# Attention and mixture of experts in one kernel: scaling of the values moved behind the gate products, list writes of the third batch put later, two gathers a step apart

## The chip, the cores and the metric

One core of a Trainium2 chip runs the whole kernel. The metric is device time in microseconds of one execution: 571.93 us is the median of three runs before the change (571.28 to 574.95). A profiled execution of the same kernel took 578.27 us; all durations below are from it.

## The reference

```python
# attention: batch 4, heads 8, seq 768, head_dim 64, n_global 8, n_local 96
scores = scale * q @ k.T                                  # per batch and head
rel    = pos[:, None] - pos[None, :]
keep   = (pos[None, :] < n_global) | ((rel >= 0) & (rel < n_local))
scores = where(keep, scores - slopes * dist, -1e9)
a      = exp(scores - max);  a = a / (sum(a) + 1e-9)
x      = (a @ v)  ->  rows of 3072 tokens x 512

# mixture of experts, one expert of 8 for each token (D 512, F 1024)
logits = x @ w_gate + modality_bias[modality_id]
e_idx  = argmax(logits);  gate_w = softmax(logits)[e_idx]
for e in range(8):
    out[e_idx == e] = gate_w * (relu(x[e_idx == e] @ w1[e]) @ w2[e])
```

The expert's matmuls run in a split form (high and low parts of both operands, three matmuls for one product).

## The kernel before, in words

The tokens are 24 blocks of 128 rows, six for each batch. The attention is a software pipeline over them: `step(n)` (L1091) works on five blocks at once. In order of TensorE's instructions it does the scores of block n in two halves (`s_mm`, L214), the transposes of block n−1's probabilities in four groups pt_0 to pt_3 (`t_mm`, L259) with a copy out of PSUM for each (`t_cp`, L266 on ScalarE, L268 on VectorE), the product with the values of block n−2 (`pv`, L280 and L292), the gate products of block n−4 (`gate_b`, L339), the transpose of block n−3's rows (`gate_a`, L330), and the sum of the gate's four quarters for block n−4 (`gate_c`, L348, added up by VectorE at L349).

Between these, VectorE finds the maxima of the scores (`mx`, eight instructions of L230, four for each half) and ScalarE takes the exponentials (`ex`, L246). `rinv` (L301 to 307) inverts the sums of the rows, which PV puts into a column beside its values, and `xr` (L310 to 323) scales the values of PV with them, out of PSUM into `xr`, and sends the rows to HBM (`x_rows`, SP's queue). PV's two PSUM tiles for a block (`x`, pool pX) have room behind the values, and `gate_b` and `gate_c` put their results there: the gate products of block n−4 go into the tile of block n−2.

At the end of each batch the routing follows, by a table of functions and steps (`at(step, function, ...)`, L999 to 1010): `route_a` makes the one-hot choice of experts, `route_b` (L376) counts tokens with two matmuls, copies the counts (`pks`, L386) and lets POOL (VectorE for the last batch) add up bases and positions (L389 to 395), `route_d` (L398) makes the reciprocal of the gate sum and turns positions into row numbers (`pf` L404, `pi` L406), and `route_c` (L409) writes one block's tokens into the sorted list in HBM (`ids_sorted`), six indirect DMAs from POOL for a batch. For the first two batches (BE = 2) they are spread over the steps, one each, behind a ScalarE instruction of the step; for the others they come together. What the table gives to steps past the attention is run by `rest()` (L1167), a generator from which `fill` takes one piece at every second turn of the first three expert units.

The experts are 14 units: three with tokens of the first two batches alone (`e0` to `e2`), eight of 256 rows (`s`) and three of 128 (`g`) with what is left. Those of the first two batches can start when the attention ends, since their lists are planned from step 17 on (`plan_e`); weights of `e0` are loaded from step 18 (LAST) on and split into high and low parts in steps 20 to 23 (`split`: ScalarE L623, VectorE L624). `ld_x` reads a unit's list (`uie`, in step 22), `gather_x` (L587) gathers its rows with two indirect DMAs from POOL (`xge`), `x_t` (L627) transposes them, and the first matmul of `e0` (L652) follows the gates of the last blocks.

What sets the order: TensorE, ScalarE and VectorE are in an order written out by hand during the attention (L1073 to 1076), TensorE and ScalarE also among the experts. POOL, SP, and VectorE's work from `rest()` on are placed by a scheduler that runs a model of the program; it can set such an instruction between others that stand ahead of it in the code.

Of the kernel before, what the change touches and what calls it, by code (L numbers as in the profile page):

```python
# [26 lines left out]
NBLK = NT // P  # L27
NG0, NL0 = 8, 96
NB = S // P
# [8 lines left out]
BE = 2  # L38
# [13 lines left out]
GE = 2  # L52
# [7 lines left out]
def bc(ap, n):  # L60
    return ap.unsqueeze(2).broadcast_to([ap.shape[0], ap.shape[1], n])
# [7 lines left out]
def moe_attention_kernel(ctx, tc, q, k, v, qs, ks, vr, vo32, n_global, n_local, modality, w_gate, mod_bias, w1, w2, out):  # L69
# [8 lines left out]
    def p_p(name):  # L78
        return psum.tile([P, 512], F32, tag="pP", name=name, bufs=2)
# [44 lines left out]
    def copyv(n):  # L124
        i, r = n % NB, n % NV
        nc.gpsimd.tensor_copy(vo[n % 3][0:64], va[r][0:64])
        if i:
            nc.gpsimd.tensor_copy(vo[n % 3][64:P], va[(n - 1) % NV][64:P])
# [94 lines left out]
    def mx(n, hh):  # L223

        if n not in blk:
            blk[n] = gp.tile([P, H], F32, tag="nmx", name=f"nmx{n}", bufs=3)
        nmx = blk[n]
        hp, h = hh // 2, hh % 2
        sc = pp.tile([P, W], F32, tag="sc", name=f"sc{n}_{hh}", bufs=8)
        V.tensor_tensor_reduce(  # L230
            out=sc,
            in0=pss[n, hp // 2][h][:, hp % 2 * W : (hp % 2 + 1) * W],
            in1=(tbl0 if n % NB == 0 else tbl)[:, hh, :],
            op0=ALU.add,
            op1=ALU.min,
            scale=-0.125,
            scalar=3.0e38,
            accum_out=nmx[:, hh : hh + 1],
        )
        scs[n, hh] = sc  # L240
# [13 lines left out]
    def t_mm(n, hp):  # L254

        pr = prs[(NP * n + hp) % NPR]
        tp = p_p(f"pt{n}_{hp}")
        for j, o in enumerate((0, P, PRW - P)):
            nc.tensor.transpose(tp[:, j * P : (j + 1) * P], pr[:, o : o + P], ident)  # L259
        pts[n, hp] = tp  # L260

    def t_cp(n, hp, act=False):
        tp = pts[n, hp]
        pT = pp.tile([P, 3, P], F32, tag="pT", name=f"pT{n}_{hp}", bufs=4)
        if act:
            last[0] = nc.scalar.copy(pT.rearrange("p a b -> p (a b)"), tp[:, 0 : 3 * P])  # L266
        else:
            V.tensor_copy(pT.rearrange("p a b -> p (a b)"), tp[:, 0 : 3 * P])  # L268
        pts[n, hp] = pT

    pxs = {}
# [29 lines left out]
    def rinv(n):  # L301

        rin = gp.tile([P, H], F32, tag="rin", name=f"rin{n}")
        for h in range(2):
            rows = pxs[n][h][:, 0 : NP * D1].rearrange("p (a d) -> p a d", d=D1)
            V.tensor_scalar_add(rin[:, h:H:2], rows[:, :, D], 1e-9)
        V.reciprocal(rin, rin)
        blk[n] = rin

    def xr(n):  # L310
        b, i = n // NB, n % NB
        px, rin = pxs[n], blk.pop(n)
        xv = gp.tile([P, DM], F32, tag="xr", name=f"xr{n}", bufs=3)
        xrs[b, i] = xv
        for h in range(2):
            V.tensor_tensor(  # L316
                xv.rearrange("p (a h d) -> p a h d", h=2, d=D)[:, :, h, :],
                px[h][:, 0 : NP * D1].rearrange("p (a d) -> p a d", d=D1)[:, :, 0:D],
                bc(rin[:, h:H:2], D),
                ALU.mult,  # L320
            )
        t0 = n * P
        nc.sync.dma_start(xd[t0 : t0 + P, :], xv)
# [20 lines left out]
    def gate_c(b, i, lq, o=NP * D1):  # L344

        if i == 0:
            lgts[b] = gp.tile([P, NB, E], F32, tag="lgt", name=f"lgt{b}")
        nc.tensor.matmul(lq[:, o : o + E], gt.pop((b, i)), sel, start=True, stop=True)  # L348
        V.tensor_add(lgts[b][:, i, :], lq[:, o : o + E], tbias[:, b * NB + i, :])  # L349
# [231 lines left out]
    def ld_x(s):  # L581
        n = P * s.halves
        so = nc.sync.value_load(s.o_src, min_val=0, max_val=E * NT)
        s.ui = idp.tile([P, 2, 2], I32, tag="ui", name=f"ui{s.name}")
        nc.sync.dma_start(s.ui[:, 0 : s.halves, :], ids[ds(so, n), 0:2].rearrange("(t p) o -> p t o", p=P))

    def gather_x(s):  # L587
        s.xg = xgp.tile([P, 2, DM], F32, tag="xg", name=f"xg{s.name}")
        for t in range(s.halves):
            nc.gpsimd.indirect_dma_start(  # L590
                out=s.xg[:, t, :],
                out_offset=None,
                in_=s.xsrc,
                in_offset=bass.IndirectOffsetOnAxis(ap=s.ui[:, t, 0:1], axis=0),
            )
# [295 lines left out]
    def at(n, f, *args):  # L891
        todo.setdefault(n, []).append((f, args))
# [106 lines left out]
    LAST = NBLK - NB  # L999
    spaced = {}  # L1000
    for b in range(B):
        n0 = b * NB
        at(n0 + NB + 3, route_a, b)
        at(n0 + NB + 4, route_b, b)
        at(n0 + NB + 4, route_d, b)
        for j in range(NB):
            if b < BE:
                spaced[n0 + NB + 5 + j] = (b, j)
            else:
                at(n0 + NB + 5, route_c, b, j)  # L1010
    at(1, consts_a)
    at(1, consts_l)
    at(2, consts_m)
# [21 lines left out]
    eslots, slist, grs = [], [], []  # L1035
# [26 lines left out]
    at(LAST, lambda: ld_w(eslots[0], "a", (0, 1)))  # L1062
    at(LAST + 1, lambda: ld_w(eslots[0], "a", (2, 3)))
    at(LAST + 4, lambda: [ld_x(s) for s in eslots])
    at(LAST + 5, lambda: [gather_x(s) for s in eslots[:GE]])
    for j in range(4):
        at(LAST + 2 + j, split, None, "a", j)
    at(LAST + 5, lambda: ld_w(eslots[0], "b"))
# [9 lines left out]
    def load(n):  # L1078

        if n + 3 < NBLK:  # L1080
            load_kq(n + 3)
        if n + LV < NBLK:
            loadv(n + LV)

    def gates(n):
        return n // NB, n % NB
# [4 lines left out]
    def step(n):  # L1091

        on, back = n < NBLK, 0 < n <= NBLK
        load(n)
        if on:
            s_mm(n, 0)
        if back:
            t_mm(n - 1, 0)
        if on:
            s_mm(n, 1)  # L1100
            for hh in (0, 2, 1, 3):
                mx(n, hh)
                ex(n, hh)
        if back:
            t_cp(n - 1, 0)
            t_mm(n - 1, 1)
            t_cp(n - 1, 1, True)
        if n in spaced:
            route_c(*spaced.pop(n), last[0])
        if on:  # L1110
            for hh in (4, 6, 5, 7):
                mx(n, hh)
                ex(n, hh)
        if n > 1:
            pv(n - 2)
            rinv(n - 2)
            xr(n - 2)
        if n > 3:
            gate_b(*gates(n - 4), pxs[n - 2][0])
        if back:  # L1120
            t_mm(n - 1, 2)
            t_cp(n - 1, 2, True)
        if n > 2:
            gate_a(*gates(n - 3))
        if back:
            t_mm(n - 1, 3)
            copyv(n - 1)
        if n > 3:
            gate_c(*gates(n - 4), pxs[n - 2][1])
        for f, args in todo.pop(n, []):  # L1130
            if f is split:
                args = (eslots[0],) + args[1:]
            if f is route_b:
                args += (pxs[n - 2][1],)
            f(*args)
        if back:
            t_cp(n - 1, 3)
        pxs.pop(n - 2, None)

    for n in range(NBLK + 1):  # L1140
# [95 lines left out]
    for u in range(nslot):  # L1236
        s = order[u]
# [137 lines left out]
```

## Time and profile before

| | us |
|---|---|
| median of three runs | 571.93 (571.28 to 574.95) |
| the profiled execution | 578.27 |
| its span, first to last instruction | 576.5 |
| attention, to the first expert matmul | 0 to 261.9 |
| experts and end | 261.9 to 576.5 |
| TensorE busy | 503.4 (87%) |
| VectorE busy | 319.2 (55%) |
| ScalarE busy | 283.3 (49%) |
| POOL busy | 137.6 (24%) |
| mean granted TensorE clock | 0.881 of full |

The span is 1.8 us shorter than the execution's time. Shares are means over two stages with different limits: in the attention five engines hand work around, among the experts TensorE works nearly without a break. A busy time of TensorE says nothing of its speed; the granted clock has to be read beside it. The steps begin, by the first score matmul of each (step 2 to step 23): 12.9, 18.8, 26.3, 35.5, 44.3, 56.4, 65.3, 74.8, 86.9, 96.4, 107.8, 116.7, 126.2, 138.2, 147.2, 157.2, 169.5, 179.1, 189.3, 198.4, 207.9, 220.5.

### The profile page before, as it was taken

The page shows a single profiled execution, that of the slowest core. Times are in us where ns is not written, and L with a number is a line of the kernel's source. Part 1 is how long each engine was busy: PE and PEld are TensorE (multiplying, and loading weights), DVE is VectorE, ACT ScalarE, POOL GpSimd, SP SyncE. Part 2 cuts the span into 40 slices and gives each one's busy share as a digit, 9 for nine tenths or more (in the row PEclk, how much of TensorE's full clock was granted, in tenths as well). Part 3 has the DMA queues.
Part 4 walks back from the last instruction along what each step waited for, and adds up shares of the span by engine and source line. Part 5 has one row for each costly group of instructions (what it writes and reads, how often), then busy time and mean ns, then how long its engine had stood idle before and what let it go on. Part 6 is the DMA issues. An engine that isn't in the chain of part 4 may idle for free.

```text
span 576.5 us, 14334 instructions
## 1 busy us (share of the span) xinstructions
PE 503.4 (87%) x5597; PEld 437.4 (76%) x5597; DVE 319.2 (55%) x971; ACT 283.3 (49%) x523; POOL 137.6 (24%) x198
## 2 busy tenths in 40 slices
PE   7869788788886884579999999998999999999990
PEld 6757677676665764468898998987898899889980
DVE  6763535544456551334978656574658565856430
ACT  6553533544435551323654555564547555865420
POOL 8211102211322115410133032152033303230100
PEclk9995857876769766559999999999999999999997
DMA  8695532534435416212857677587668867696100
GB/s 274 215 308 185 152 124 89 162 116 131 137 111 169 162 51 203 95 67 70 290 162 250 207 261 243 194 306 254 222 217 281 300 205 252 233 324 188 69 21 22
DMA packets 59396, 105.52 MB, mean 183 GB/s; under 512 B 9615, under 2 KB 23335, under 8 KB 59320
## 3 DMA queue, kind: packets, MB, share of 16 engines
q1 hardware_dynamic: 54552, 91.47, 49.2%
q0 software_dynamic: 4768, 13.05, 6.1%
q8 instruction: 46, 0.75, 0.5%
q14 instruction: 30, 0.25, 0.1%
HBM read 90.13 MB, written 14.63 MB: 182 GB/s over the span
## 4 chain that ended last, share of the span: by engine, by line
PE 59%; DVE 14%; issue 13%; DMA 5%; ACT 3%; POOL 2%; SPq 0%; POOLq 0%; ACTq 0%; DVEq 0%; another core or an unknown queue 0%
PE pt L259 9%; PE s L214 6%; PE phs L654 4%; PE phs L652 4%; PE phs L653 4%; PE x L280 3%; DMA uig<-ids_sorted 3%; DVE sc L230 3%; PE x L292 3%; DVE pT L268 3%; PE pos L696 3%; PE pos L695 3%; PE pos L694 3%; PE phe L652 2%; PE phe L653 2%
## 5 line engine op out<-in xcount | busy, mean ns | idle before, releaser
L246 ACT ACTIVATE pr<-sc,nmx 128x168 f32<-128x168 f32 x192 | 67.6, 423 | 64.1 <-DVE nmx L230 63.1
L259 PE MATMUL pt<-ident,pr 128*128 128x128 f32 x288 | 66.2, 352 | 18.8 <-DVE pT L268 14.7
L653 PE MATMUL phs<-xls,ahs 128*128 128x256 f32 x256 | 72.2, 282 | 1.3 <-DVE xls L639 1.3
L654 PE MATMUL phs<-xhs,als 128*128 128x256 f32 x256 | 72.6, 284 | 0.6 <-DVE als L624 0.5
L652 PE MATMUL phs<-xhs,ahs 128*128 128x256 f32 x256 | 72.2, 282 | 0.0
L259 PEld LDWEIGHTS pt<-ident,pr 128*128 128x128 f32 x288 | 37.7, 171 | 32.8 <-issue 17.7
L590 POOL DMA_INDIRECT xgs<-x_rows,uis x16 | 30.2, 1888 | 133.8 <-DMA uis<-ids_sorted 79.4
L230 DVE CUSTOM_DVE_ANT_0 sc<-s,tbl 128x168 f32<-128x168 f32 x192 | 52.2, 327 | 8.8 <-PE s L214 7.6
L214 PE MATMUL s<-kt,qt 64*64 64x128 f32 (+1 forms) x1536 | 56.2, 295 | 0.5 <-DMA kt<-in_ks 0.4
L214 PEld LDWEIGHTS s<-kt,qt 64*64 64x64 f32 x1536 | 50.2, 166 | 6.8 <-issue 5.7
L694 PE MATMUL pos<-bhs,hhs 128*128 128x512 f32 x128 | 51.4, 401 | 0.0
L696 PE MATMUL pos<-bhs,hls 128*128 128x512 f32 x128 | 50.6, 395 | 0.0
L268 DVE COPY pT<-pt 128x384 f32<-128x384 f32 x48 | 26.5, 553 | 43.4 <-PE x L292 43.4
L695 PE MATMUL pos<-bls,hhs 128*128 128x512 f32 x128 | 50.5, 395 | 0.0
L412 POOL DMA_INDIRECT ids_sorted<-tki,pi x24 | 25.1, 1044 | 105.7 <-ACT pr L246 51.5
L653 PEld LDWEIGHTS phs<-xls,ahs 128*128 128x128 f32 x256 | 48.8, 191 | 1.9 <-DVE xls L639 1.6
L654 PEld LDWEIGHTS phs<-xhs,als 128*128 128x128 f32 x256 | 48.8, 191 | 1.3 <-DVE als L624 1.3
L659 DVE SCALAR_TENSOR_TENSOR hls<-phs,hhs 128x512 fp32r<-128x512 f32 x32 | 22.1, 692 | 49.0 <-ACT hhs L658 49.0
L652 PEld LDWEIGHTS phs<-xhs,ahs 128*128 128x128 f32 x256 | 48.9, 191 | 0.4
L266 ACT COPY pT<-pt 128x384 f32<-128x384 f32 x48 | 22.9, 478 | 47.7 <-PE x L292 33.4
L658 ACT ACTIVATE hhs<-phs 128x512 fp32r<-128x512 f32 x32 | 19.1, 598 | 51.9 <-PE phs L654 43.4
L339 PE MATMUL x<-xT,wg 128*32 128x128 f32 x184 | 11.8, 335 | 35.4 <-DVE xr L316 33.0
(338 smaller groups left out, 1189.0 us busy)
## 6 DMA issues: line engine op xcount, KB each, us to landing
va<-in_vr SPq DMA_DIRECT2D x25, 260.0 KB
qt<-in_qs SPq DMA_DIRECT2D x24, 256.0 KB
x_rows<-xr SPq DMA_DIRECT2D x24, 256.0 KB
kt<-in_ks SPq DMA_DIRECT2D x20, 288.0 KB
vl<-in_vo SPq DMA_DIRECT2D x50, 81.2 KB
rawe0a<-in_moe_w SPq DMA_DIRECT2D x4, 512.0 KB
rawe0b<-in_moe_w SPq DMA_DIRECT2D x4, 512.0 KB
rawe1a<-in_moe_w SPq DMA_DIRECT2D x4, 512.0 KB
```

The source lines that it names most:

```text
L214: nc.tensor.matmul(ps[h][64 * half : 64 * half + 64, c : c + cnt], qt[hs, hp, 64 * half : 64 * half + 64], keys, start=True, stop=True,)
L230: V.tensor_tensor_reduce(out=sc, in0=pss[n, hp // 2][h][:, hp % 2 * W : (hp % 2 + 1) * W], in1=(tbl0 if n % NB == 0 else tbl)[:, hh, :], o ...
L246: last[0] = nc.scalar.activation(pr[:, h * (PRW - W) : h * (PRW - W) + W], scs.pop((n, hh)), AF.Exp, bias=blk[n][:, hh : hh + 1], scale=-1.0,)
L259: nc.tensor.transpose(tp[:, j * P : (j + 1) * P], pr[:, o : o + P], ident)
L268: V.tensor_copy(pT.rearrange("p a b -> p (a b)"), tp[:, 0 : 3 * P])
L590: nc.gpsimd.indirect_dma_start(out=s.xg[:, t, :], out_offset=None, in_=s.xsrc, in_offset=bass.IndirectOffsetOnAxis(ap=s.ui[:, t, 0:1], axi ...
L652: nc.tensor.matmul(o, hi[:, fs], s.xh[:, c, :], start=(c == 0), stop=False)
L653: nc.tensor.matmul(o, hi[:, fs], s.xl[:, c, :], start=False, stop=False)
L654: nc.tensor.matmul(o, lo[:, fs], s.xh[:, c, :], start=False, stop=(c == 3))
L694: nc.tensor.matmul(s.po[t], s.hh[:, fc, tt], hi[:, wv], start=(fc == 0), stop=False)
L695: nc.tensor.matmul(s.po[t], s.hh[:, fc, tt], lo[:, wv], start=False, stop=False)
L696: nc.tensor.matmul(s.po[t], s.hl[:, fc, tt], hi[:, wv], start=False, stop=(fc == 7))
```

## The change

```diff
@@ the table
-        at(n0 + NB + 4, route_d, b)
+        at(n0 + NB + 4 if b < BE else max(n0 + NB + 4, NBLK + 1), route_d, b)
...
-                at(n0 + NB + 5, route_c, b, j)
+                at(max(n0 + NB + 5, NBLK + 1), route_c, b, j)
...
-    at(LAST + 5, lambda: [gather_x(s) for s in eslots[:GE]])
+    for j in range(GE):
+        at(LAST + 5 + j, lambda j=j: gather_x(eslots[j]))
@@ step(n)
         if n > 1:
             pv(n - 2)
-            rinv(n - 2)
-            xr(n - 2)
         if n > 3:
             gate_b(*gates(n - 4), pxs[n - 2][0])
         if back:
             t_mm(n - 1, 2)
-            t_cp(n - 1, 2, True)
+            t_cp(n - 1, 2)
         if n > 2:
             gate_a(*gates(n - 3))
         if back:
             t_mm(n - 1, 3)
+            t_cp(n - 1, 3, True)
             copyv(n - 1)
         if n > 3:
             gate_c(*gates(n - 4), pxs[n - 2][1])
+        late = []
         for f, args in todo.pop(n, []):
             if f is split:
                 args = (eslots[0],) + args[1:]
             if f is route_b:
-                args += (pxs[n - 2][1],)
+                f(*args, pxs[n - 2][1])
+            else:
+                late.append((f, args))
+        if n > 1:
+            rinv(n - 2)
+            xr(n - 2)
+        for f, args in late:
             f(*args)
-        if back:
-            t_cp(n - 1, 3)
```

So in each step: `rinv` and `xr` of block n−2 come behind the gate's work instead of ahead of it; the copy of pt_2 goes from ScalarE to VectorE and that of pt_3 from VectorE to ScalarE, right behind its transposes; of the routing, `route_b` stays ahead of `rinv`, and the rest of the step's table comes behind `xr`. For the third batch, `route_d` goes from step 22 and `route_c` from step 23 to step 25, which is past the attention and so in `rest()`. The gather of `e1` goes from step 23 to step 24. The last block's code behind the loop is as it was.

VectorE at the end of step 6, before: the last of eight maxima, `rinv` and `xr` of block 4, the gate's sum, the copy of pt_3, and the next step's first maximum.

```order
L230 ISA sc_7_1114,nmx_1084<-s_1_1_1067,tbl_161 128x168
L230 ISA nmx_1084 128x1
L306 TENSOR_SCALAR rin_1151<-x_0_1117 128x4
L306 TENSOR_SCALAR rin_1151<-x_1_1118 128x4
L307 RECIPROCAL rin_1151<-rin_1151 128x8
L316 TENSOR_TENSOR xr_1155<-x_0_1117,rin_1151 128x4x64
L316 TENSOR_TENSOR xr_1155<-x_1_1118,rin_1151 128x4x64
L349 TENSOR_TENSOR lgt_867<-x_1_1118,tbias 128x8
L268 COPY pT_3_1187<-pt_3_1178 128x384
L230 ISA sc_0_1236,nmx_1235<-s_0_0_1195,tbl 128x168
```

And now:

```order
L230 ISA sc_7_1114,nmx_1084<-s_1_1_1067,tbl_161 128x168
L230 ISA nmx_1084 128x1
L268 COPY pT_2_1161<-pt_2_1157 128x384
L349 TENSOR_TENSOR lgt_861<-x_1_1118,tbias 128x8
L306 TENSOR_SCALAR rin_1180<-x_0_1117 128x4
L306 TENSOR_SCALAR rin_1180<-x_1_1118 128x4
L307 RECIPROCAL rin_1180<-rin_1180 128x8
L316 TENSOR_TENSOR xr_1184<-x_0_1117,rin_1180 128x4x64
L316 TENSOR_TENSOR xr_1184<-x_1_1118,rin_1180 128x4x64
L230 ISA sc_0_1236,nmx_1235<-s_0_0_1195,tbl 128x168
```

The copy and the gate's sum have come ahead of `rinv` and `xr`; the copy is that of pt_2.

VectorE at the end of step 22, before: the gate's sum, the third batch's counts (`pks`), its reciprocals, `pf` and `pi`, a split of `e0`'s weights, the copy of pt_3, the next step's first maximum.

```order
L349 TENSOR_TENSOR lgt_3759<-x_1_3693,tbias 128x8
L386 COPY pks_3764<-x_1_3693 128x96
L400 TENSOR_REDUCE se_3777<-ex_3601 128x6
L401 TENSOR_SCALAR se_3777<-se_3777 128x6
L402 RECIPROCAL tki<-se_3777 128x6
L404 TENSOR_REDUCE pf_3781<-pos_3773 128x6
L406 CAST pi_3783<-pf_3781 128x6
L624 TENSOR_TENSOR ale_3819<-rawe0a_3290,ahe_3818 128x1024
L268 COPY pT_3_3822<-pt_3_3753 128x384
L230 ISA sc_0_3865,nmx_3864<-s_0_0_3824,tbl 128x168
```

And now, at the end of the step after it, step 23, where `pf` and `pi` of the third batch stand, up to the copy of pt_0 in step 24:

```order
L268 COPY pT_2_3933<-pt_2_3929 128x384
L349 TENSOR_TENSOR lgt_3753<-x_1_3890,tbias 128x8
L306 TENSOR_SCALAR rin_3952<-x_0_3889 128x4
L306 TENSOR_SCALAR rin_3952<-x_1_3890 128x4
L404 TENSOR_REDUCE pf_4248<-pos_3767 128x6
L307 RECIPROCAL rin_3952<-rin_3952 128x8
L406 CAST pi_4250<-pf_4248 128x6
L316 TENSOR_TENSOR xr_3956<-x_0_3889,rin_3952 128x4x64
L316 TENSOR_TENSOR xr_3956<-x_1_3890,rin_3952 128x4x64
L624 TENSOR_TENSOR ale_3964<-rawe0a_3294,ahe_3963 128x1024
L268 COPY pT_0_3979<-pt_0_3975 128x384
```

`pf` and `pi` have moved by one step, into the middle of `rinv` and `xr` of block 21; the reciprocals have gone to step 21.

POOL from the last copy of values to the gather of `e2`, before:

```order
L128 COPY vo_80<-va_76 64x520
L590 DMA xge_3972<-x_rows,uie_3794 128x512 x2
L590 DMA xge_3975<-x_rows,uie_3805 128x512 x2
L389 TENSOR_TENSOR base<-base,pks_3764 128x8 x6
L393 TENSOR_TENSOR pos_3773<-pks_3764,base 128x48
L391 COPY base<-base 128x8
L394 TENSOR_TENSOR pos_3773<-pos_3773,ebase 128x48
L395 TENSOR_TENSOR pos_3773<-pos_3773,oh_3607 128x48
L412 DMA ids_sorted<-tki,pi_3783 24832x16 x6
L590 DMA xge_4295<-x_rows,uie_3816 128x512 x2
```

And now:

```order
L128 COPY vo_80<-va_76 64x520
L389 TENSOR_TENSOR base<-base,pks_3758 128x8
L590 DMA xge_3960<-x_rows,uie_3788 128x512 x2
L590 DMA xge_4058<-x_rows,uie_3799 128x512 x2
L389 TENSOR_TENSOR base<-base,pks_3758 128x8 x5
L393 TENSOR_TENSOR pos_3767<-pks_3758,base 128x48
L391 COPY base<-base 128x8
L394 TENSOR_TENSOR pos_3767<-pos_3767,ebase 128x48
L395 TENSOR_TENSOR pos_3767<-pos_3767,oh_3609 128x48
L412 DMA ids_sorted<-tki,pi_4250 24832x16 x6
L590 DMA xge_4277<-x_rows,uie_3810 128x512 x2
```

One of the six sums of bases has gone ahead of the four gathers; the gathers of `e0` and `e1` still stand together, and the six list writes where they stood.

## Rows read from the trace of the kernel before

**Rows 1.** The page's second part, one row: the TensorE clock that was granted in 40 equal slices of the span (14.4 us each), in tenths of full speed (9 is 90% or more).

```profile
PEclk9995857876769766559999999999999999999997
```

**Rows 2.** The table by stretches: stretch and its length in us, busy us and (instructions) of each engine, granted clock as a share of 2.4 GHz, mean busy share of the DMA engines, GB/s. Steps 2 to 4; steps 5 to 21; from step 23's scores to the first expert matmul; the experts.

```profile
12.80:35.40 22.60, 17.74 (x441) 14.60 (x439) 15.81 (x81) 13.48 (x37) 5.30 (x9) 1.00 0.78 246
35.40:207.80 172.40, 140.24 (x2625) 118.23 (x2623) 84.98 (x467) 79.12 (x207) 35.73 (x64) 0.76 0.47 147
220.40:261.90 41.50, 25.52 (x332) 20.75 (x332) 12.64 (x46) 9.01 (x21) 14.53 (x22) 0.59 0.40 135
261.90:566.00 304.10, 298.70 (x1872) 265.44 (x1871) 191.71 (x298) 166.98 (x217) 68.25 (x50) 1.00 0.64 214
```

**Rows 3.** Who waited for whom: engine, line waited at, what ended the wait: us in total, times, longest us. Two rows of TensorE's waits from 0 to 262 us, and one of VectorE's from the whole span.

```profile
PE x L339 <- DVE xr L316: 33.0, 19, 3.8
PE pt L259 <- DVE pT L268: 14.7, 8, 8.3
...
DVE pf L404 <- POOL pos L395: 13.4, 3, 8.9
```

**Rows 4.** Timeline of TensorE at the end of step 4 and in step 5, mostly at full clock: start in us from the span's start, duration in us, engine, line, operation, tiles (out<-in), shape, count, and in brackets the idle time before it and what ended it. Scores `s`, first PV group `x` (L280), gate products (L339), third transpose group `pt` of the step's second half, next step's scores.

```profile
33.35 0.43 PE L339 MATMUL x<-xT,wg 128*32 128x128 f32 x8 [1.80 <-DVE xr L316]
...
35.48 0.91 PE L214 MATMUL s<-kt,qt 64*64 64x128 f32 x32
...
38.12 0.70 PE L280 MATMUL x<-vl,pT 40*64 40x65 f32 x32
...
41.70 0.43 PE L339 MATMUL x<-xT,wg 128*32 128x128 f32 x8 [1.80 <-DVE xr L316]
...
43.23 0.90 PE L259 MATMUL pt<-ident,pr 128*128 128x128 f32 x3 [0.19 <-ACT pT L266]
...
44.29 0.51 PE L214 MATMUL s<-kt,qt 64*64 64x128 f32 x4
```

**Rows 5.** Timeline of VectorE and ScalarE in the same step 5: first score row `sc`, copy `pT` of pt_0 on VectorE and of pt_1 on ScalarE, the second four exponentials `pr`, `rinv` and `xr`, the copy `lps`.

```profile
37.44 0.32 DVE L230 CUSTOM_DVE_ANT_0 sc<-s,tbl 128x168 f32<-128x168 f32 x1
...
39.25 0.56 DVE L268 COPY pT<-pt 128x384 f32<-128x384 f32 x1 [0.72 <-PE x L292]
...
39.53 0.48 ACT L266 COPY pT<-pt 128x384 f32<-128x384 f32 x1 [0.31 <-PE x L292]
...
40.09 1.41 ACT L246 ACTIVATE pr<-sc,nmx 128x168 f32<-128x168 f32 x4
...
40.73 0.22 DVE L306 TENSOR_SCALAR rin<-x 128x4 f32<-128x4 f32 x2
...
41.22 0.76 DVE L316 TENSOR_TENSOR xr<-x,rin 128x256 f32<-128x256 f32 x2
...
42.20 0.27 ACT L341 COPY lps<-x 128x128 f32<-128x128 f32 x1 [0.70 <-PE x L339]
```

**Rows 6.** Timeline of TensorE in a step at half clock, step 9: its scores, its gate products, the next step's scores.

```profile
74.81 1.55 PE L214 MATMUL s<-kt,qt 64*64 64x128 f32 x32
...
83.72 0.65 PE L339 MATMUL x<-xT,wg 128*32 128x128 f32 x8 [1.21 <-DVE xr L316]
...
86.89 0.51 PE L214 MATMUL s<-kt,qt 64*64 64x128 f32 x4
```

**Rows 7.** Timeline of VectorE in step 10, the routing of the first batch: the copy `pks`, and `pf`, which reads POOL's positions.

```profile
96.54 0.26 DVE L386 COPY pks<-x 128x96 f32<-128x96 f32 x1 [0.33 <-PE x L384]
...
99.58 0.20 DVE L404 TENSOR_REDUCE pf<-pos 128x6 f32<-128x48 f32 x1 [2.24 <-POOL pos L395]
```

**Rows 8.** Timeline of steps 22 and 23: step 22's scores; the last list write of the second batch, first and last of four gathers, the last of the third batch's position sums; `pf`, a weight split and the copy of pt_3 on VectorE; the transposes on TensorE that use its tile.

```profile
207.87 1.55 PE L214 MATMUL s<-kt,qt 64*64 64x128 f32 x32
...
216.08 0.98 POOL L412 DMA_INDIRECT ids_sorted<-tki,pi  x1 [8.90 <-ACT pr L246]
...
222.87 1.00 POOL L590 DMA_INDIRECT xge<-x_rows,uie  x1 [3.42 <-DMA uie<-ids_sorted]
...
226.69 0.95 POOL L590 DMA_INDIRECT xge<-x_rows,uie  x1 [0.30 <-issue]
...
230.00 0.28 POOL L395 TENSOR_TENSOR pos<-pos,oh 128x48 f32<-128x48 f32 x1
230.31 0.20 DVE L404 TENSOR_REDUCE pf<-pos 128x6 f32<-128x48 f32 x1 [8.94 <-POOL pos L395]
...
230.72 1.23 DVE L624 TENSOR_TENSOR ale<-rawe0a,ahe 128x1024 fp32r<-128x1024 f32 x1
...
231.86 0.55 DVE L268 COPY pT<-pt 128x384 f32<-128x384 f32 x1
...
232.56 0.87 PE L259 MATMUL pt<-ident,pr 128*128 128x128 f32 x3 [8.35 <-DVE pT L268]
```

**Rows 9.** Timeline of the attention's end: pt_2 of the last block on TensorE, the last `rinv` on VectorE, the first expert matmul.

```profile
252.38 0.90 PE L259 MATMUL pt<-ident,pr 128*128 128x128 f32 x3
...
261.33 0.23 DVE L306 TENSOR_SCALAR rin<-x 128x4 f32<-128x4 f32 x2 [3.09 <-ACT lps L341]
...
261.92 0.36 PE L652 MATMUL phe<-xhe,ahe 128*128 128x256 f32 x1
```

**Rows 10.** Timeline among the experts: the gather of the first unit of the last plan on POOL, and the first transposes that use it.

```profile
309.72 0.98 POOL L590 DMA_INDIRECT xgs<-x_rows,uis  x1 [14.25 <-DMA uis<-ids_sorted]
...
329.55 0.60 PE L635 MATMUL mts<-ident,xgs 128*128 128x128 f32 x4
```

## The prediction

> **What bounds the kernel now.** I read the clock row of the page first, then a table by stretches, then who TensorE waited for, and last one step of the attention instruction by instruction. In the clock row [rows 1] the reader sees full clock (2.4 GHz) in the first slices, a mixture from the fourth to the eighteenth, and full clock again from then on. The table [rows 2] puts names to it: the mixture of experts (261.9 to 566) has TensorE busy 298.7 of 304.1 us at a granted clock of 1.00, so nothing but fewer matmuls would shorten it, and the change takes none away. The attention runs at 0.76, and its end, 220.4 to 261.9, has TensorE busy for 25.5 of 41.5 us. So all that can be won lies ahead of 262 us. There TensorE's largest wait is for `xr` of VectorE, 33.0 us in 19 times, 1.74 each [rows 3]: the gate products (L339) write the PSUM tile that `xr` reads.
>
> One step at full clock [rows 4]: step 5 starts at 35.48, its gate products start at 41.70 after a wait of 1.80, and from gate products to the next step's scores it took 2.13 in the step before (33.35 to 35.48). That is 6.22 + 2.13 = 8.35 us. (Step 5 itself took 8.81, since the clock fell in its last part.) A step at 1.2 GHz [rows 6] takes 12.08 with a wait of 1.21, so 10.9 without. The 17 steps from 35.48 to 207.87 take 172.4 us, 10.14 each: a mixture of the two.
>
> **The change part by part.** *`rinv` and `xr` behind the gate products.* No instruction is added or dropped; a PSUM copy changes engines with another of the same size (0.56 on VectorE, 0.48 on ScalarE [rows 5]). TensorE's own order stays, and the wait of 1.80 goes, since the tile that the gate products write has no reader yet. What is late next, in step 5 counted from 35.48: PV ended at 4.42 (41.70 less 1.80). The last transpose group, pt_3, needs pt_2's copy; that now stands on VectorE behind the second four score rows, which end at 5.25 (40.73), so it is done at 5.81. TensorE gets there by itself at 4.42 + 1.34 = 5.76 (41.70 to 43.23 less the old wait of 0.19): no loss. gate_c needs the copy `lps`, which stands on ScalarE behind four exponentials that end at 6.02 (41.50), so it is there at 6.29; 0.3 for gate_c, and the next step's scores start at some 6.65 instead of 8.35. I take 6.9, for hand-overs between engines that I cannot see. Bounds: 6.65, and 8.9 if the clock stays a mixture (10.14 less 1.74, plus 0.5 for the new waits).
>
> The clock is the larger half of this. Before it fell, at the end of step 5, TensorE had stood still 1.80 and 0.19 us in one step [rows 4]; from 12.8 to 35.4 it kept 1.00 with TensorE busy 17.7 of 22.6 us [rows 2]. A step of 6.65 would hold some 0.3 us of waiting, a fuller engine than in that stretch. So I expect full clock in most steps. Bounds: never falling, or the mixture as before.
>
> `xr` then ends 1.25 us (40.73 to 41.98) after gate_c's sum, at about 8.2, that is 1.5 into the next step; VectorE's next score rows come at 2.0 of that step (37.44 against 35.48 by the same spacing), so VectorE is not late. Its DMA, `x_rows`, is 1.2 us later, and the loads behind it on SP's queue with it; they are made one to three steps ahead, and the traffic of 147 GB/s [rows 2] becomes some 216 at 6.9 us a step, below the 246 that the first steps drew.
>
> Steps with more work cost more. In steps 10 and 16 VectorE waits for POOL's positions: 13.4 us in three, less 8.9, makes 2.2 each [rows 3], and from `pks` to `pf` it takes 3.0 [rows 7]. `pks` now stands ahead of `rinv`, so about 1 us of waiting is left, but score rows follow at once: 0.17 + 3.04 + 0.4 after 6.9 puts them at 10.5 instead of 8.7; I take 2.0 a step. Steps 9, 15, 20, 21 have routing sums or a weight split of 1.23 on VectorE behind `xr`: 1.0 each. And I let the clock fall twice after such steps, each for a step's length: 10.9 less 6.9, 4.0 each. Sum of the 17 steps: 117.3 + 4 + 4 + 8 = 133.3, a gain of 39.1. Step 4 adds its wait, 1.7.
>
> *Third batch's list writes.* Before, VectorE's `pf` in step 22 stood from 221.3 to 230.3 for POOL, whose position sums lay behind four gathers that waited for the list [rows 8]; the transposes behind it started only at 232.56. In the new order `pf` is gone from step 22, but not from the attention: the scheduler puts it into step 23, between that step's `rinv` and `xr`. On POOL nothing moves: gathers, sums and six list writes stand as they did, except that one of six sums goes ahead of the gathers. What then comes late, from step 22's start (207.87 before): the list write waits for ScalarE's copy, done at 4.5 (40.01 in step 5), 4.6; the list is read back 6.8 later (216.08 to 222.87), 11.4; from there to the last position 7.4 (230.28), 18.7. VectorE gets to `pf` at 7.8 (step 22 with its split) + 7.1 = 14.9 and waits 3.8. Then `pf`, reciprocal, `pi`, `xr` and the split, about 2.9 with their hand-overs, and the copy of pt_0, 0.5: 22.1, which step 24's pt_2 needs. From pt_2 to the first expert matmul it was 252.38 to 261.92 [rows 9], 9.5 at mostly half clock; I take 8.4 (at full clock it would be near 6). First expert matmul at 30.5 instead of 54.05 (207.87 to 261.92): a gain of 23.5. Bounds: 27 if `pf` waits for nothing, 36 if it waits 8.9 as before.
>
> *Gathers a step apart.* POOL has them back to back in both orders: nothing.
>
> *Behind the attention.* The route of the third batch takes two more turns of the planner, 5 us at 1.3 a piece. The first list of the last plan was gathered at 309.72 and used at 329.55 [rows 10], so this hides; I charge 1.0. A split of 1.23 has come ahead of the last `rinv` on VectorE, in a chain at the end of the attention: 1.0.
>
> Sum: 39.1 + 1.7 + 23.5 − 2.0 = 62.3. The profiled execution took 578.27 us, 6.3 above the median of 571.93; it becomes 516.0, and the median about 510.
>
> **The rivals.** *The clock keeps swinging.* For it: from 35.4 to 207.8 it did so in every step or two, and after the change short waits for copies remain in each. Against it: the stretch at 1.00 named above. Price: 8.9 a step gives 17 × 1.24 = 21.1 (its extras are in the 10.14), step 4 1.7, the end 4 less, 19.5, and −2: a gain of 40.3, 532 us. The Trainium skill tells of such a case (TensorE: Matmul & The Clock Gate, "A second HAM failure mode: psum-queue depth-cycling"): where PSUM buffers turn over in each iteration, small idles between groups of matmuls keep the clock swinging. By that rule the change would leave the swing, as its tiles still turn over each step, and the time would be this rival's; the trace bears it out from 35.4 on, and not from 12.8 to 35.4.
>
> *The third batch's part does not do what it says.* `pf` in step 23 may wait as long as it did in step 22. For it: POOL's order is the same. Against it: VectorE comes to it a step later. Price: 36 instead of 30.5, 515 us.
>
> *Slower.* The place is the PSUM pair of PV: a step's PV may start only when `xr` of two steps before has read it. By my reckoning `xr` ends 1.5 into a step and PV starts at 2.64 (38.12 less 35.48), 1.1 to spare; before, at full clock, 4.5 (8.35 + 2.64 less 6.50, where `xr` ended). `rinv` now waits for ScalarE's `lps` too, as it did for 3.09 us in the one place where the old order had it so [rows 9]. If `xr` came d late, each of 18 steps would grow by d less 1.1. The gain of 62 is used up at d = 4.6; at 5.2 the time is 571.9 − 62.3 + 18 × 4.1 = 583. Nothing in the rows holds `lps` that long.
>
> **How the numbers follow.** A measurement of this kernel can tell about 1% from no change. Forecast 0.62; swinging clock 0.20 (532); long `pf` 0.12 (515); slower 0.03 (583); no change that can be told 0.03. Low end: 17 × 6.65 without falls of the clock saves 12.3 more, the end at 27 saves 3.5: 494. High end: the swinging clock, 532, with 2 for hand-overs: 534. Faster is 0.94, within 1% 0.03, slower 0.03.
>
> **What would show it.** Right: TensorE's wait for `xr` is gone from the list; a plain step takes about 7 us; the clock row shows nines to the end of the attention, with a lower slice or two; step 22's `pf` is gone and one in step 23 waits some 4 us; the first expert matmul comes near 200 us; the stretch of the experts is as long as before to 3 us. Wrong: PV waits for `xr`; fives in the clock row; TensorE idle among the experts for a list that comes late.

## The result and the profile after

The changed kernel takes 496.02 us (median of 4 runs, 494.71 to 499.26), the one before took 573.44 in the same session: ratio 0.866, interval 0.861 to 0.872. Taken a second time, in another session (c1 below), it took 496.16 us, 0.867 (0.863 to 0.871). The profiled execution took 494.71 us, with a span of 492.9 us; the span before was 576.5.

The clock row of the page, of the changed kernel (a slice is 12.3 us), to be set beside [rows 1]:

```profile
PEclk9999999999999899999999999999999999999995
```

The fives to eights of before are gone but for one slice (the last one is where the work runs out). The table by stretches, with the columns of [rows 2]: steps 2 to 4, steps 5 to 21, from step 22's scores to the first expert matmul (in [rows 2] this stretch starts a step later, with step 23's scores), the experts:

```profile
12.80:32.20 19.40, 17.89 (x441) 14.73 (x439) 15.04 (x77) 13.08 (x36) 5.11 (x9) 1.00 0.78 249
32.20:149.80 117.60, 110.47 (x2625) 90.23 (x2623) 84.10 (x467) 73.25 (x207) 35.17 (x63) 1.00 0.69 218
149.80:181.00 31.20, 24.91 (x489) 19.84 (x489) 20.25 (x82) 16.63 (x39) 17.68 (x28) 0.89 0.55 188
181.00:485.00 304.00, 297.86 (x1871) 265.11 (x1870) 191.60 (x297) 165.55 (x215) 67.91 (x50) 0.99 0.64 216
```

The reader sees the same number of matmuls in steps 5 to 21 (2625) in 117.6 us instead of 172.4, at a clock of 1.00 instead of 0.76; TensorE is busy for 94% of it. By parts, in us:

| part of the span | before | after | gain | predicted |
|---|---|---|---|---|
| up to step 5's scores | 35.48 | 32.28 | 3.2 | 1.7 |
| steps 5 to 21 | 172.39 | 117.61 | 54.8 | 39.1 |
| step 22's scores to the first expert matmul | 54.05 | 31.02 | 23.0 | 23.5 |
| experts to the end | 314.6 | 312.0 | 2.6 | −2.0 |
| span | 576.5 | 492.9 | 83.6 | 62.3 |

TensorE's waits over the whole span (line waited at, what ended it: us in total, times, longest), to be set beside [rows 3]:

```profile
PE pt L259 <- DVE pT L268: 8.4, 26, 1.3
PE x L280 <- DVE xr L316: 3.6, 1, 3.6
```

The 33.0 us at the gate products have no row any more. What is left is mostly 0.2 to 0.3 us a time for copies (the longest 1.3), and one wait of PV for `xr`. A plain step of the changed kernel, that is one without routing, planning or weight splits on VectorE, is step 14; on TensorE (scores, PV, gate products, pt_3, next scores), against [rows 4]:

```profile
92.92 0.91 PE L214 MATMUL s<-kt,qt 64*64 64x128 f32 x32
...
95.56 0.70 PE L280 MATMUL x<-vl,pT 40*64 40x65 f32 x32
...
97.27 0.42 PE L339 MATMUL x<-xT,wg 128*32 128x128 f32 x8
...
98.82 0.55 PE L259 MATMUL pt<-ident,pr 128*128 128x128 f32 x3 [0.21 <-DVE pT L268]
...
99.46 0.91 PE L214 MATMUL s<-kt,qt 64*64 64x128 f32 x32
```

and on VectorE the first instructions that it does within this step (`rinv` and `xr` of the step before), and its copy of pt_2, against [rows 5]:

```profile
93.11 0.22 DVE L306 TENSOR_SCALAR rin<-x 128x4 f32<-128x4 f32 x2
...
93.61 0.76 DVE L316 TENSOR_TENSOR xr<-x,rin 128x256 f32<-128x256 f32 x2
94.28 0.32 DVE L230 CUSTOM_DVE_ANT_0 sc<-s,tbl 128x168 f32<-128x168 f32 x1
...
98.21 0.56 DVE L268 COPY pT<-pt 128x384 f32<-128x384 f32 x1
```

The step is 6.54 us long (99.46 less 92.92) with one wait of 0.21. `xr` ends 1.45 into it (94.37), PV, which needs the PSUM pair that `xr` reads, starts at 2.64: 1.2 to spare. The one long wait stands in the attention's end (before: [rows 8, 9]):

```profile
165.22 0.95 POOL L590 DMA_INDIRECT xge<-x_rows,uie  x1 [0.30 <-issue]
165.26 0.22 DVE L306 TENSOR_SCALAR rin<-x 128x4 f32<-128x4 f32 x2
...
168.52 0.20 DVE L404 TENSOR_REDUCE pf<-pos 128x6 f32<-128x48 f32 x1 [3.04 <-POOL pos L395]
...
169.28 0.76 DVE L316 TENSOR_TENSOR xr<-x,rin 128x256 f32<-128x256 f32 x2 [0.28 <-DVE pi L406]
169.76 1.46 PE L280 MATMUL x<-vl,pT 40*64 40x65 f32 x32 [3.60 <-DVE xr L316]
...
180.91 0.36 PE L652 MATMUL phe<-xhe,ahe 128*128 128x256 f32 x1
```

`pf`, which stands between `rinv` and `xr`, waits for POOL, whose last gather and sums come first; PV waits for `xr`. PV's 32 matmuls then take 1.46 instead of 0.70: the clock is at half from 167.8, within the wait, to 174.6, the only time between 32 and 181 us.

### The profile page after: what moved, and what is told of

Read it like the earlier page. It is cut to its first block, busy times and chain, and to the rows that moved or that the text cites. A ratio compares the mean times of both kernels' runs of the same rounds, so it can differ in the third digit from the quotient of the medians.

```text
span 492.9 us, 14301 instructions
## 1 busy us (share of the span) xinstructions
PE 460.7 (93%) x5597; PEld 398.3 (81%) x5597; DVE 318.6 (65%) x971; ACT 276.9 (56%) x523; POOL 137.5 (28%) x198
## 4 chain that ended last, share of the span: by engine, by line
PE 56%; DVE 16%; issue 14%; DMA 6%; ACT 3%; POOL 3%; SPq 1%; POOLq 0%; DVEq 0%
PE pt L259 6%; PE s L214 5%; PE phs L654 5%; PE phs L652 4%; PE phs L653 4%; DVE sc L230 4%; DVE pT L268 4%; DMA uig<-ids_sorted 4%; PE pos L696 3%; PE pos L695 3%; PE pos L694 3%; PE phe L652 2%; PE x L280 2%; PE phe L653 2%; PE phe L654 2%
## 5 line engine op out<-in xcount | busy, mean ns | idle before, releaser
L259 PE MATMUL pt<-ident,pr 128*128 128x128 f32 x288 | 52.5, 292 | 10.1 <-DVE pT L268 8.4
L659 DVE SCALAR_TENSOR_TENSOR hls<-phs,hhs 128x512 fp32r<-128x512 f32 x32 | 22.1, 692 | 49.4 <-ACT hhs L658 49.4
L259 PEld LDWEIGHTS pt<-ident,pr 128*128 128x128 f32 x288 | 30.0, 141 | 23.0 <-DVE pT L268 15.1
L214 PE MATMUL s<-kt,qt 64*64 64x128 f32 (+1 forms) x1536 | 44.0, 250 | 0.7 <-DMA kt<-in_ks 0.4
L214 PEld LDWEIGHTS s<-kt,qt 64*64 64x64 f32 x1536 | 38.5, 132 | 5.7 <-issue 4.5
L710 POOL DMA_INDIRECT out<-obs,ois x16 | 16.1, 1006 | 47.4 <-ACT obs L709 44.4
```

The source lines that it names most:

```text
L214: nc.tensor.matmul(ps[h][64 * half : 64 * half + 64, c : c + cnt], qt[hs, hp, 64 * half : 64 * half + 64], keys, start=True, stop=True,)
```

## The experiments

Theory A: the wait of TensorE for `xr` in each step cost twice, by itself and by the clock that fell after it; the move of `rinv` and `xr` takes both away; the rest of the change is worth a few us. Rivals: the third batch's part carries the gain (B), the exchange of the copies does (C), the clock's fall has nothing to do with the wait (D). From e5 on the letters are those of each run's own expectation.

**e1_step_only: the changed step, the rest as before.**

```diff
-        at(n0 + NB + 4 if b < BE else max(n0 + NB + 4, NBLK + 1), route_d, b)
+        at(n0 + NB + 4, route_d, b)
-                at(max(n0 + NB + 5, NBLK + 1), route_c, b, j)
+                at(n0 + NB + 5, route_c, b, j)
-    for j in range(GE):
-        at(LAST + 5 + j, lambda j=j: gather_x(eslots[j]))
+    at(LAST + 5, lambda: [gather_x(s) for s in eslots[:GE]])
```

Expected: 

> The changed step (scaling behind the gate products, the copies of pt_2 and pt_3 exchanged) with the table of the routing and the gathers as before the change. Theory A (TensorE's standing still for xr in each step costs its own length and, through the clock, as much again): plain steps of 6.5 us at full clock as in the changed kernel, pf back in step 22 with a wait of 7 to 9 us: 502 us. Theory B (the gain comes from the third batch's part): 540 us or more, plain steps of 9 us.

Measured: 500.19 us (498.68 to 504.64), ratio 0.873 (0.868 to 0.878). A plain step takes 6.54. Its end, timeline of VectorE and TensorE:

```profile
162.69 0.43 PE L339 MATMUL x<-xT,wg 128*32 128x128 f32 x8
...
168.55 0.20 DVE L404 TENSOR_REDUCE pf<-pos 128x6 f32<-128x48 f32 x1 [8.13 <-POOL pos L395]
...
171.71 0.90 PE L259 MATMUL pt<-ident,pr 128*128 128x128 f32 x3 [8.59 <-DVE pT L268]
...
184.28 0.36 PE L652 MATMUL phe<-xhe,ahe 128*128 128x256 f32 x1
```

So the step alone gives all but some 4 us, by medians of two sessions; the intervals of the ratios (0.861 to 0.872 for the whole change) overlap. `pf` waits 8.13 here, nearly as long as before (8.94 [rows 8]), and yet from step 22's scores (149.72) to the first expert matmul it is 34.6 instead of 54.05. Before, the transposes that waited stood ahead of step 23's PV; here PV and the gate products (162.69) are done before the wait, since the copy that stands behind `pf` is a later one. After the wait 12.6 us were left, before it was 29.4 (232.56 to 261.92 [rows 8, 9]), at half clock for much of it and with more waits for `xr`.

**e2_table_only: the kernel before with those three edits alone** (the diff above the other way round).

Expected: 

> The kernel before with only the table and the gathers changed (route_d and route_c of the third batch at step 25, gathers a step apart), the steps as before. Theory A: the steps from 5 to 21 stay at 10.1 us each, only the end can move: 566 to 573 us. Theory B: 540 us or less.

Measured: 569.47 us (564.86 to 574.86), ratio 0.991 (0.987 to 0.995). Its waits and its clock:

```profile
PE x L339 <- DVE xr L316: 38.5, 21, 6.8
```

```profile
PEclk9977585885855787769999999999999999999996
```

B falls: 4.5 us by itself, some 4 on top of the new step. One of its waits for `xr` is now 6.8 long, behind `pf`, which waits 7.2 itself. In the profile the end does gain: from step 22's scores (214.16) to the first expert matmul (257.31) it takes 43.15 instead of 54.05. But steps 5 to 21, whose order on TensorE, ScalarE and VectorE these edits do not touch, took 178.9 instead of 172.4 in this execution, with the clock at half for more of the time.

**e3_scale_back: the changed kernel with `rinv` and `xr` ahead of the gate products again.**

```diff
             pv(n - 2)
+            rinv(n - 2)
+            xr(n - 2)
...
-        if n > 1:
-            rinv(n - 2)
-            xr(n - 2)
```

Expected: 

> The changed kernel with rinv and xr put back ahead of the gate products; the exchange of the copies, the order of the routing's functions, the table and the gathers stay changed. Theory A: the gate products wait for xr again, 1.8 us a step at full clock, and the clock swings: steps of some 10 us, 560 to 570 us. Theory C (what helped is that pt_3's copy no longer stands on VectorE behind the scaling and the routing): steps near 7, 500 to 510 us.

Measured: 561.56 us (559.42 to 564.93), ratio 0.979 (0.973 to 0.984). Its waits, and the stretch of its steps 5 to 21:

```profile
PE x L339 <- DVE xr L316: 39.0, 21, 5.9
```

```profile
34.50:208.50 174.00, 144.16 (x2623) 121.53 (x2622) 86.66 (x467) 79.65 (x208) 35.71 (x64) 0.74 0.47 146
```

So the place of two calls holds 65.5 of the 77 us. The exchange of the copies stays in this kernel, and its 17 steps take 174.0, before 172.4: C falls. Whether the two calls would give as much without the exchange, no run shows. The 12 us that this kernel keeps come from the end, which takes 36.75 (208.53 to 245.28). There the parts of the change overlap: of the 23.0 us that the end gains with all of them, the step alone gives 19.5 (e1), the table alone 10.9 (e2), the table with the exchanged copies 17.3 (this run).

**e4_filled_wait: the kernel before, with TensorE given work in the wait.**

```diff
-    def t_mm(n, hp):
+    def t_mm(n, hp, times=1):
...
+        for _ in range(times):
...
+        if back:
+            t_mm(n - 1, 2, 4 if n > 3 else 1)
         if n > 3:
             gate_b(*gates(n - 4), pxs[n - 2][0])
```

(The later call of `t_mm(n - 1, 2)` is dropped. The same transposes are done four times over; nothing is left out.)

Expected: 

> The kernel before, its order of VectorE and ScalarE untouched; on TensorE the transposes of pt_2 come ahead of the gate products and are done four times over into the same tile (three times for nothing), so that TensorE works in its wait for xr. Theory A (what makes the clock fall is that TensorE stands still): full clock in most of the attention, a step of some 8.1 us (8.35 less what pt_2 took behind the gate), 17 steps gain 35: 535 us. Theory D (the clock swings with the transposes too, only the removal of the wait counts): steps of 9.5 or more, 565 us or more, as three more groups of transposes lengthen a step at half clock.

Measured: 540.18 us (537.01 to 540.35), ratio 0.938 (0.934 to 0.943). TensorE in a step (scores, the twelve transposes, gate products, next scores; line numbers are one higher in this kernel), and two stretches of the table: 17 steps, from the second half of step 5's scores to that of step 22's, and the first five of them:

```profile
58.82 0.91 PE L214 MATMUL s<-kt,qt 64*64 64x128 f32 x32
...
63.20 1.53 PE L260 MATMUL pt<-ident,pr 128*128 128x128 f32 x12
65.05 0.43 PE L340 MATMUL x<-xT,wg 128*32 128x128 f32 x8 [0.31 <-DVE xr L317]
...
66.84 0.91 PE L214 MATMUL s<-kt,qt 64*64 64x128 f32 x32
```

```profile
36.00:183.90 147.90, 132.81 (x2778) 110.01 (x2776) 85.55 (x465) 77.41 (x209) 35.49 (x64) 0.97 0.54 167
36.00:78.00 42.00, 39.52 (x884) 32.76 (x882) 24.77 (x136) 23.49 (x64) 6.79 (x11) 1.00 0.63 200
```

`xr` is as late as before and the step as full of other things, but TensorE works through 1.5 of the wait and stands 0.31. The clock holds, and a plain step takes 8.02 (66.84 less 58.82) against 6.54 in the changed kernel: 1.5 for the wait itself. D falls. (Over the 17 steps the clock is at 0.97; it still fell twice, in steps 11 and 17, behind the routing of steps 10 and 16.) The 17 steps take 172.4 us before, 147.8 here (36.09 to 183.90) and 117.6 in the changed kernel, so of its 54.8 us there some 25 are what the filled wait gives back and 30 the wait and the rest. (A little of the 25 is not the clock: at full clock the prediction read 8.35 a step from [rows 4], 0.33 more than here, where pt_2's transposes no longer come behind the gate products.) The PSUM tiles turn over here as often as in the kernel before, so that alone does not make the clock swing. The rule of the Trainium skill that stood behind the first rival (TensorE: Matmul & The Clock Gate, "A second HAM failure mode: psum-queue depth-cycling") names the turnover and the small idles together. This run and the changed kernel, at 1.00 from 32 to 150 us with the same turnover, put it on the idles. Which feature of the idles counts, the length of one or how they follow each other, is not shown: from 12.8 to 35.4 us the kernel before kept 1.00 [rows 2] through waits of up to 1.80.

**e6_scale_twice and e7_scale_4x: how late may `xr` be?** The changed kernel with `xr`'s multiplies repeated (`* 4` in the second):

```diff
-        for h in range(2):
+        for h in list(range(2)) * 2:
             V.tensor_tensor(
```

Expected of the first: 

> The changed kernel with the two multiplies of `xr` done twice over in each step (the same result written again, 0.76 us more of VectorE ahead of its release of the PSUM pair). Nothing is left out. In the changed kernel `xr` ends 1.45 us into a step and PV, which needs the pair, starts at 2.64: 1.2 to spare. Theory A (spare time as read there; what stands behind `xr` on VectorE is not late either): 0.76 hides, a plain step stays at 6.5 to 6.6, 496 to 500 us at a mean clock of 0.97 or more. Theory B (VectorE paces the step, so all that it gets is paid): 6.54 + 0.76 = 7.3 a step, 22 steps, 513 us or more.

Expected of the second: 

> The changed kernel with the two multiplies of `xr` done four times over in each step (2.3 us more of VectorE ahead of its release of the PSUM pair). Nothing is left out. Theory A (PV waits once `xr` is later than the 1.2 us to spare): PV waits 1.1 us in each step, a plain step takes 7.6 at full clock; 22 steps by 1.1 make 24, 520 us, if the clock stays; and since TensorE then stands 1.1 in one piece each step, the clock may swing again, which would make it 535 to 560. A wait of TensorE for `xr` is back in the list of waits, now at PV (L280), not at the gate products. Theory B (VectorE paces the step): 8.8 a step, 545 us or more, with waits for score rows and copies in the list and none for `xr`. Theory C (all of it hides): 496 to 500.

Measured: 506.57 us (504.83 to 507.09), ratio 0.884 (0.881 to 0.887), and 523.49 (521.56 to 526.74), 0.915 (0.911 to 0.919). `xr` of e6 takes 1.42, of e7 2.74, so it is 0.66 and 1.98 later. A plain step takes 6.54 and 7.36. The first hides, as A had it. For the second, step 12 (`xr`, PV, the next step's PV), and the table for the better part of steps 6 to 10:

```profile
89.46 2.74 DVE L316 TENSOR_TENSOR xr<-x,rin 128x256 f32<-128x256 f32 x8
91.92 1.01 PE L280 MATMUL x<-vl,pT 40*64 40x65 f32 x32 [0.43 <-DVE xr L316]
...
99.29 1.01 PE L280 MATMUL x<-vl,pT 40*64 40x65 f32 x32 [0.44 <-DVE xr L316]
```

```profile
42.20:78.00 35.80, 32.34 (x762) 26.33 (x762) 31.33 (x149) 18.88 (x56) 6.43 (x11) 1.00 0.64 199
```

PV starts 0.5 later in the step, with a wait of 0.43, and from there to the gate products it takes 0.3 longer: 0.82 in all, so 1.16 of the 1.98 had been spare. The price line of the rival "slower" (d less 1.1 a step) holds to 0.1. (The expectation had `xr` 2.3 later, and so a wait of 1.1 and a step of 7.6.) In these steps the clock stays at 1.00 with a wait of 0.43 in each; it was at half from 80.7 to 84.1, behind the routing of step 10. What A missed is e6's total, 10 us over the changed kernel: 6.5 of its span are lost in steps 5 to 21, in those with routing or planning on VectorE (step 16 takes 7.81 instead of 7.15) and by the clock, which was at half for 10 us in step 18 (123.6 to 133.8); and 4.3 at the end.

**e5_rows_late: `pf` out of step 23.**

```diff
+    for f, args in [t for t in todo[NBLK + 1] if t[0] is route_d]:
+        f(*args)
+    todo[NBLK + 1] = [t for t in todo[NBLK + 1] if t[0] is not route_d]
     l1_first(3)
```

Expected: 

> The changed kernel, with the third batch's row positions (`route_d`: the sums of exponentials and `pf` with its cast) recorded at the very end of the hand-written order, so that they can no longer stand in step 23 between that step's `rinv` and `xr`. Nothing is left out. In the changed kernel `pf` there waits 3.04 us for POOL, so `xr` is late and PV of step 24 stands 3.60 us; right after it TensorE's clock is at half from 167.8 to 174.6. Theory A (that wait is what the end of the attention still pays): the wait of PV for `xr` goes, the clock stays full to the first expert matmul, which comes 3.6 us earlier for the wait and some 3 earlier for the clock: 489 to 492 us, first expert matmul 24 to 26 after step 22's start instead of 31.0. Theory B (another link of the end, the list read back for the experts' rows or the transposes of the first gathered rows, is as late): 495 to 497, with TensorE's wait moved to the first expert's transposes. Theory C (the positions are wanted for the last plan, and come too late there): over 500, with a wait among the experts.

Measured: 493.61 us (489.76 to 494.41), ratio 0.861 (0.857 to 0.864). PV of step 24 waits for nothing, but the clock falls a step earlier, after waits in step 22; transposes, step 23's scores, PV, the first expert matmul:

```profile
155.90 0.55 PE L259 MATMUL pt<-ident,pr 128*128 128x128 f32 x3 [1.26 <-DVE pT L268]
...
158.96 1.55 PE L214 MATMUL s<-kt,qt 64*64 64x128 f32 x32
...
170.42 1.01 PE L280 MATMUL x<-vl,pT 40*64 40x65 f32 x32
...
179.79 0.36 PE L652 MATMUL phe<-xhe,ahe 128*128 128x256 f32 x1
```

From step 22's scores (149.86) to the first expert matmul it is 29.9 instead of 31.0. So half of A came true: the wait of 3.6 is gone, but A had 24 to 26 for the end and 489 to 492 in all. The clock is at half for 10 us here (157.6 to 167.8) against 7 in the changed kernel, and the end keeps only 1.1 of the 3.6.

**e8_gathers_together: the changed kernel with the gathers in one step** (the last part of the first diff).

Expected: 

> The changed kernel with the first experts' four gathers recorded together again, as before the change, instead of a step apart. Nothing is left out. Theory A (the list that they need is read back only in step 23, so POOL has them back to back in either order): 495 to 498, no difference that can be told. Theory B (the step apart lets POOL's sums for the third batch go ahead of the last gathers, so `pf` waits longer without it): the wait of `pf` in step 23 grows from 3.0 to some 7, PV is late by as much, 500 to 503.

Measured: 499.97 us (495.42 to 501.8), ratio 0.871 (0.867 to 0.876). The total is B's, but its place is refuted: `pf` waits 1.4 us in step 23, not 7, PV's wait is 2.0, no longer than in the changed kernel, and the end takes 31.3 (153.66 to 184.93) as there. The time went in steps 17 and 18, which took 20.0 us instead of 16.3, with the clock at half for 10 us. In step 17 TensorE waited longer for the copy of pt_2; first the changed kernel, then this run:

```profile
119.18 0.55 PE L259 MATMUL pt<-ident,pr 128*128 128x128 f32 x3 [1.26 <-DVE pT L268]
```

```profile
114.91 0.62 POOL L128 COPY vo<-va 64x520 f32<-64x520 f32 x1 [1.61 <-DMA ids_sorted<-tki,pi]
...
118.21 0.20 DVE L404 TENSOR_REDUCE pf<-pos 128x6 f32<-128x48 f32 x1 [2.95 <-POOL pos L395]
...
120.28 0.55 PE L259 MATMUL pt<-ident,pr 128*128 128x128 f32 x3 [2.32 <-DVE pT L268]
```

By the profile a copy of values on POOL waited for a list write of the first batch; the second batch's position sums stand behind that copy, `pf` behind the sums, and the copy of pt_2 behind `pf`. The clock fell at 121.5. Whether the edit or chance made the list write late, and so moved the median, two more runs were to tell.

**c1_changed_again and e9_late_together**: the changed kernel once more, and beside it e5 and e8 in one.

Expected of the first: 

> The changed kernel once more, unaltered, on the same chip as the next kernel, so that differences of less than 1% (the gathers together, 499.97; the rows late, 493.61) can be set against it. Theory A (those differences are where TensorE's clock happens to fall after a step with more work, not the edits): 494 to 500 us, with the step after step 22's start to the first expert matmul at 31 again and the clock at half for some 7 us in the attention, in the steps from 15 on. Theory B (the edits did it): 496 within 1, between the two.

Expected of the second: 

> The changed kernel with both small edits: the third batch's row positions at the end of the hand-written order, and the four gathers recorded together. Nothing is left out. Theory A (late rows are worth the 3.6 us that PV stood, less what the clock takes back elsewhere; the gathers are worth nothing): 490 to 495, no wait of PV for `xr`. Theory B (the gathers together cost some 4 us, as the one median of 499.97 would have it): 497 to 500. Theory C (neither edit does anything): as the changed kernel on the same chip, within 1 us.

Measured: 496.16 us (494.79 to 497.06) and 491.70 (489.86 to 497.16), ratios 0.867 (0.863 to 0.871) and 0.862 (0.856 to 0.867). The profile of the first has the wait of 3.7 again and 31.0 for the end; its time fits both of its theories. That of the second has no wait of PV, 25.7 for the end, and there the clock:

```profile
151.90:177.70 25.80, 22.85 (x489) 17.95 (x488) 19.66 (x77) 16.56 (x39) 13.47 (x21) 1.00 0.59 206
```

It fell in steps 17 and 18 instead (120.0 to 130.3), after a wait of 1.87 in step 17. So the gathers together cost nothing that can be told beside the late rows (e5's edit), which are worth 2 to 5 us: both kernels that have them have medians under 494, both takes of the changed kernel 496, with intervals that overlap. Whether e8's 499.97 is chance stays open.

## Why the prediction came out as it did

The mechanism held: the wait for `xr` and the clock's fall after it were the cost, and moving two helpers took both. The median, 496.02, lies 14 us under the forecast of 510 and near the low end of 494, which had no falls of the clock. The sum was 21.3 us short of the span's gain, 15.7 of it in the term for steps 5 to 21:

- *Plain step, 6.9 against 6.54.* The working came to 6.65, and 0.25 was added for hand-overs. The trace shows one wait, 0.21, ahead of pt_3, and TensorE reaches gate_c 6.29 into the step (99.21), the very time that the working has. 17 steps: 6.1 us.
- *Two falls of the clock, 8.0 against none.* In these 17 steps it did not fall; it did once later, behind step 22. In e8 and e9, whose code for these steps is the same, it fell once in them, with 3 to 4 us lost there, so that it fell not once is in part luck.
- *Steps with more work, 8.0 against 6.4*, nearly right as a sum and wrong in its places. Steps 9, 15, 20 and 21, priced at 1.0 each, cost 0.05 in all. The routings of steps 10 and 16, whose `pf` falls in TensorE's steps 11 and 17, cost 1.3 and 2.5 (priced 2.0 each); step 5 cost 0.5. Steps 18 and 19, the planning for the experts, cost 2.1 and had no price.
- *Up to step 5, 1.7 against 3.2.* 1.5 came in step 4, 1.7 in steps 2 and 3, which had no term (step 2 starts at 12.89 in both).
- *The end, 23.5 against 23.0.* `pf` waited 3.04 instead of 3.8. But the number stood under the third batch's list writes, and e1 shows 19.5 of it without them, e2 10.9 by them alone, so the step by itself brings most of it. The upper bound held: 36 "if `pf` waits 8.9 as before" was 34.6 in e1 (8.13). Of 27 "if `pf` waits for nothing" e9 gave 25.7, but e5, where the clock fell, 29.9. The wait did not pass through the copy of pt_0 to pt_2, as the working said, but through `xr` to PV: pt_2 of step 24 came 23.8 after step 22's start (173.67) instead of 22.1, and from there to the first expert matmul it took 7.2 instead of 8.4. That these two misses nearly cancel is luck.
- *Behind the attention, −2.0 against 2.6.* No wait of TensorE for a list is in the rows. From the first expert matmul to the end it is 311.0 to 313.1 us in the changed kernel and e1 to e4; the 314.6 of before was a little long, for reasons not looked at.

Of the rivals, the swinging clock fell (0.76 to 1.00), and with it the reading that the turnover of the tiles alone keeps the clock swinging. The slower one had the right place, PV behind a late `xr`: it came true once, by 3.6 us, not 18 times. 1.2 to spare is what the rows show, 1.1 was predicted. (The prediction calls it the `xr` of two steps before; in the rows, and in its own numbers, it is that of the step before. And `x_rows` comes 1.7 us later by its working, 8.2 less 6.50, not 1.2. Nothing hangs on either.)

## What to carry to other kernels

Where the granted clock swings in a stretch with a short wait in every loop, price the wait twice (here some 30 us for itself and what came with it, and some 25 for the clock), and test it before any reordering by filling the wait with repeated work. Ask of each reader of a PSUM tile which write comes next into that tile: a reader placed behind it costs nothing until the next turn of the tile, and the spare time is read from the timeline (here 1.2 of 6.54 us, confirmed by delaying the reader). Spare time in the plain steps is not spare in the few that carry extra work, and a short wait of another engine placed between two halves of one chain (`rinv`, `pf`, `xr`) is paid by whoever waits for the end of the chain. And where two edits shorten the same end, their gains do not add: test each alone.

## What was not expected of the hardware

More work made the kernel before faster: nine extra transposes in each step, with pt_2's own moved into the wait, took 33.8 us off its 573.9. And the clock's falls moved about between kernels whose work there is the same: at half from some 167 to 174 in both takes of the changed kernel, from 158 to 168 in e5, from 122 to 132 in e8 (and twice more from 162 on) and from 120 to 130 in e9; from 120 to 132 the changed kernel keeps 1.00. Each of these followed a wait of TensorE of over 1 us (the fall of e7 at 80.7 did not: its waits there were 0.2 to 0.4), and not each such wait was followed by a fall. In step 17 it waited 1.26 and 1.40 in the two takes of the changed kernel, 1.36 in e5 and 1.86 in e1, without a fall; 1.87 in e9 and 2.32 in e8, with one. In step 22 it waited 1.02 in the changed kernel without a fall, and 1.26 in e5 with one. With the wait ahead of it such a fall costs 2 to 4 us (3.7 in e8's steps 17 and 18), as much as the small edits that one would judge by these totals.
